# Order of the first chunk: tile 3's scores behind tile 1's product with v, a lower pace of the channel mix, and tile 1's v ahead of the fourth block of w_k

## The chip, the cores and the metric

The kernel runs on one core of a Trainium2 chip. The metric is the device time of one execution in microseconds (us). The kernel before was timed in three runs; one further execution was recorded by the hardware profiler.

## What is computed

Four batches of eight heads, 768 positions, head width 64; a biased local attention, and on its output a gated channel mix over the 512 joined features. Inputs are float32 (the weights are given as 64-bit words that the kernel turns into float32 itself).

```python
scores = q @ k.T / 8 + bias        # bias: -slope[h] * distance
scores = where(keep, scores, -1e9) # keep: first 8 keys, or 0 <= i - j < 96
a = exp(scores - max); a = a / (sum(a) + 1e-9)
x = a @ v                          # joined over heads: (4, 768, 512)
x_prev = x shifted by one position
xk = mu_k * x + (1 - mu_k) * x_prev
xr = mu_r * x + (1 - mu_r) * x_prev
k = maximum(xk @ w_k, 0)           # w_k 512 x 1024
out = sigmoid(xr @ w_r) * ((k * k) @ w_v)   # w_r 512 x 512, w_v 1024 x 512
```

## The kernel before

The work is cut into 24 tiles of 128 positions (6 to a batch). A step of the main loop (L658 and after) handles one tile in four quarters, `hp` 0 to 3. For a tile the scores are computed on TensorE (`scores`), the softmax on three engines (`softmax`: VectorE adds the bias and takes the maximum at L375, ScalarE takes the exponential at L376, VectorE the sum plus 1e-9 and its reciprocal at L389 and L390, GpSimd scales at L393), then the result is transposed and multiplied by v. The product with v of a tile is issued two steps after its scores (`weighted`, L473 and L487); its copy into `x` is at L496. Tiles 0 to 3 (`HEAD` is 4) use plain 128-key blocks, are transposed on TensorE (L453) and take their data from tiles loaded at the start; later tiles use a window of 168 keys, are transposed on VectorE (L410, L411) and go through a small DRAM buffer.

Two tiles make a chunk of 256 positions for the channel mix, 12 chunks in all (0 to 11). `ffn(c)` mixes x with its shifted copy (xk and xr; for chunk 0 in `plain_mix`, ScalarE at L521 and VectorE at L522) and returns a generator, `channel_mix`, whose parts are issued turn by turn: kp (x by w_k, L564), z (x by w_r, L542), vps (the squares by w_v, L597). Chunk 0 multiplies whole float32 words; the later chunks split each number into a high and a low part and use three products (L533 to L535). A budget counts the turns that the main loop grants: `run_ffn(2.5)` twice in each quarter, and -17.5 at the start of chunk 0, which is queued in step 3 (`LAG`).

The weights are 20 blocks of 128 x 512: 8 of w_k, 4 of w_r, 8 of w_v. `weight_load` issues the DMA of a block (L163, 0.5 MB) into a place named by `w_homes`, which must be free of its earlier use. `weight_begin` makes a float32 word of it: one step on ScalarE (even blocks, L178) or GpSimd (odd ones, L176) and three on VectorE (L179 to L181). `weight_split` makes the high part (ScalarE at L188, or GpSimd) and the low part (VectorE, L190 or L197) for the chunks after the first. `w_due` says how many blocks are loaded and begun by each quarter.

The order of instructions on each engine comes from a planner that takes the program's order as priority and its own estimate of times; `tc.issue_after(ins)` holds every instruction of a block that is on the engine of `ins` behind `ins`. Every engine works through its instructions in order. SyncE (SP) issues the DMAs in its own order.

Of the kernel before, what the change touches and what calls it, by code (L numbers as in the profile page):

```python
# [35 lines left out]
def tile_biased_attention_channel_mix(ctx: ExitStack, tc: tile.TileContext, qT, kT, v, n_sizes, mu_kr, w_k, w_v, w_r, q_rows, k_rows, v_rows, slopes, out):  # L36
# [108 lines left out]
    w_steps = [(name, src, k, c) for name, src, kts, n in (("k", w_k, 4, DF), ("r", w_r, 4, DM), ("v", w_v, 8, DM)) for c in range(0, n, 512) for k in range(kts)]  # L145

    w_raw = {}
    w_due = ((2, 3, 4, 5, 6, 6, 7, 7, 8, 8, 9, 9, 10, 11, 12, 13, 14, 16, 18, 20, 20, 20, 20, 20), (0, 1, 2, 3, 4, 4, 5, 5, 6, 6, 7, 7, 8, 8, 9, 10, 11, 12, 14, 16, 18, 20, 20, 20))

    def weight_load(i):  # L150
        name, src, k, c = w_steps[i]
# [12 lines left out]
        w_raw[i] = raw  # L164

    w_both = {}
    w_homes = ["xk_hi", "xr_hi", "xk_lo", "xr_lo", "kk_hi", "kk_hi", "kk_lo", "kk_lo"] + 2 * ["t4k", "t4k", "t4k", "xk_lo", "xr_lo"] + ["kk_lo", "kk_lo"]

    def weight_begin(i):
        name, src, k, c = w_steps[i]  # L170
# [12 lines left out]
    def weight_split(i):  # L183

        name, src, k, c = w_steps[i]
        word, hi = w_word.pop((name, k, c)), w_hi[name][:, k, c : c + 512]
        lo = w_low[name, k, c] = w_pool.tile([128, 512], F32R, tag="wl", name=f"w{name}_lo_{i}")
        (act.copy if i % 4 < 2 else pool_copy)(hi, word)  # L188
        if not gates:
            vec.tensor_sub(lo, word, hi)  # L190
        else:
            with ExitStack() as behind:
                if i == 8:
                    hold.extend(gates[-1:] + freed[-2:])
                for ins in hold or gates[-1:]:
                    behind.enter_context(tc.issue_after(ins))
                vec.tensor_sub(lo, word, hi)  # L197

    w_count = [0, 0, 0]
    marks = {}  # L200

    def weights_load(n):
        while w_count[2] < min(n, len(w_steps)):
# [2 lines left out]

    def weights_go(begun):
        weights_load(begun)
        with ExitStack() as behind:
            for ins in marks.values():  # L210
                behind.enter_context(tc.issue_after(ins))
            while w_count[0] < min(begun, len(w_steps)):
                weight_begin(w_count[0])
                w_count[0] += 1

    def splits_go(n):
        while w_count[1] < n:
# [5 lines left out]


    state = {}
    seen = {}
    room = r_pool.tile([128, 12, 512], F32, name="room")
    turned = room[:, 4:7].rearrange("p b x -> p (b x)").rearrange("p (l x) -> p l x", l=6)
    landed = room[:, 0:4].rearrange("p a (k x) -> p a k x", k=2)
# [73 lines left out]
    def window_tables():  # L303
        misc = q_pool.tile([128, 1024], F32, name="misc", tag="qh")
        table = q_pool.tile([128, H, WIN], BF16, name="patw", tag="qh")
        pool.memset(misc[0:32, 0:512], 0.0)
        pool_copy(table[:, :, 0:GMAX], pat[:, :, 0:GMAX])
        pool_copy(table[0:64, :, GMAX:WIN], pat[0:64, :, 32:192])
        pool_copy(table[64:128, :, GMAX:WIN], pat[64:128, :, 96:256])
        return misc[0:32, 0:512], misc[:, 512 : 512 + HH * GMAX].rearrange("p (h k) -> p h k", h=HH), table  # L310

    def scores(n, hp):
# [49 lines left out]
    def softmax(n, hp, j, units, w, p):  # L362
        s = state[n]
        for i, ps in units:
            for u in range(2):
                h = 2 * i + u
                o = ps[:, u * 256 : u * 256 + w]
                if n >= HEAD:
                    slot = 8 + 2 * j + i // 2
                elif n < HEAD - 3:  # L370
                    slot = 5 + (4 * (n - HEAD + 4) + 3 + i) % 7
                else:
                    slot = i + (4 if (HEAD - n) % 2 else 8)
                e = room[:, slot, 256 * u : 256 * u + 256]
                seen_max = vec.tensor_tensor_reduce(out=e[:, :w], in0=o, in1=p[:, h, :], op0=ALU.add, op1=ALU.min, scale=-0.125, scalar=3.0e38, accum_out=s["nmax"][:, h : h + 1])  # L375
                act.activation(e[:, :w], e[:, :w], AF.Exp, bias=s["nmax"][:, h : h + 1], scale=-1.0, accum_out=s["sum"][:, h : h + 1])  # L376
                s["e"][h] = e
        if n >= HEAD and j:
            freed.append(seen_max.ins)
        if j is None and hp % 2 == 0:  # L380
            return
        r = s_pool.tile([128, 4], F32, name=f"r_{n}_{hp}_{j}", tag="r", bufs=8)
        if j is not None:
            heads = (2 * j, 2 * j + 1, 2 * j + 4, 2 * j + 5)
            total = s["sum"].rearrange("p (a j u) -> p j a u", a=2, j=2)[:, j]
        else:
            heads = range(2 * hp - 2, 2 * hp + 2)
            total = s["sum"][:, 2 * hp - 2 : 2 * hp + 2].rearrange("p (a u) -> p a u", a=2)
        vec.tensor_scalar(r.rearrange("p (a u) -> p a u", a=2), total, 1.0e-9, None, op0=ALU.add)  # L389
        vec.reciprocal(r, r)  # L390
        for i, h in enumerate(heads):
            e = s["e"][h]
            pool.tensor_scalar(e[:, :w], e[:, :w], r[:, i : i + 1], 1.0, op0=ALU.mult, op1=ALU.mult)  # L393

    def turn(n, j):
        if n < HEAD:
# [60 lines left out]
    def weighted(n, hp):  # L457
# [6 lines left out]
        if n < HEAD:  # L464
            blocks = [state[n - 1]["va"], s["va"]] if t else [s["va"]]
            nb = len(blocks)
            et = s.pop(("et", hp))
            for u in range(2):
                h = 2 * hp + u
                o = s["av"][64 * u : 64 * u + 64, hp * 128 : (hp + 1) * 128]  # L470
                for k, vt in enumerate(blocks):
                    c = (u * nb + k) * 128
                    pe.matmul(o, vt[:, h * 64 : (h + 1) * 64], et[:, c : c + 128], start=k == 0, stop=k == nb - 1)  # L473
        else:
            lo, hi = slice(0, 64), slice(64, 128)
            every, own, back = slice(0, 4), 1, 0
            first, second = [("va", own, every), ("vb", back, slice(0, 2))], [("vb", back, every), ("va", own, slice(2, 4))]
            if not t:
                first = second = [("va", own, every)]
            for k in range(len(first)):  # L480
                for u in range(2):
                    h = 2 * hp + u
                    c = 32 * (HH * (hp % 2) + 2 * (hp // 2) + u)
                    for rows, bank, parts in ((lo, "av", first), (hi, "av2", second)):
                        vt, kind, a = parts[k]
                        o = s[bank][64 * u : 64 * u + 64, hp * 128 + 32 * a.start : hp * 128 + 32 * a.stop]
                        pe.matmul(o, s[vt][rows, h * 64 : h * 64 + 64], landed[rows, a, kind, c : c + 32], start=k == 0, stop=k == len(first) - 1)  # L487
# [28 lines left out]
    def plain_mix(xc, xp, tag):  # L516

        m, m1 = mu[tag]
        x = f_pool.tile([128, 4, 256], F32, name=f"x{tag}_0", tag=f"x{tag}_hi")
        for j in range(4):  # L520
            act.activation(x[:, j, :], xp[:, j, :], AF.Copy, scale=m1[:, j : j + 1])  # L521
            vec.scalar_tensor_tensor(x[:, j, :], xc[:, j, :], m[:, j : j + 1], x[:, j, :], op0=ALU.mult, op1=ALU.add)  # L522
        return x

    def channel_mix(xk, xr, out_rows, f_pool, f2_pool, ps_f, first=False, last=False):
# [11 lines left out]
        def z_of(i):  # L537
            z = ps_f.tile([128, 512], F32, name="z", tag="f")
            c = slice(i * 128, (i + 1) * 128)
            for k in range(4):  # L540
                if first:
                    pe.matmul(z, xr[:, k, c], w_word["r", k, 0], start=k == 0, stop=k == 3)  # L542
                else:
                    three(z, xr[0][:, k, c], xr[1][:, k, c], w_hi["r"][:, k, :], w_low["r", k, 0], k == 0, k == 3)
                    splits_ok[0] = len(w_steps)
# [5 lines left out]
        for fp in range(4):  # L551
# [17 lines left out]
                        yield  # L569
            kk = f2_pool.tile([128, 2, 256], F32, name="kk", tag="f2")  # L570
            pv = ps.rearrange("p (a q) -> p a q", a=2)
            act.activation(kk, pv, AF.Relu)  # L572
            if first:
                vec.tensor_mul(kk_all[:, 2 * fp : 2 * fp + 2, :], pv, kk)
            else:
# [33 lines left out]

    splits_ok = [0]  # L610
    gates = []
    freed = []
    hold = []
    waiting = []

    def ffn(c):
# [4 lines left out]
        elif c:  # L621
            xk, xr = (mix(xt[:, :, 1:257], xt[:, :, 0:256], tag, p4k, f_pool) for tag in "kr")
        else:
            xk, xr = (plain_mix(xt[:, :, 1:257], xt[:, :, 0:256], tag) for tag in "kr")
        return channel_mix(xk, xr, lambda i: out[(2 * c + i) * 128 : (2 * c + i + 1) * 128, :], f_pool, f2_pool, ps_f, c == 0, c == NCHUNK - 1)


    LAG = 3
    queue = []
    budget = [0.0]  # L630

# [15 lines left out]
    for step in range(NTILES + 1):  # L647
        if step + 2 < HEAD:
            load_tile(step + 2)
        if step < NTILES:  # L650
            load_v(step)
        if step == HEAD - 1:
            vg, kg, patw = window_tables()
        for hp in range(4):
            if hp == 0 and step > 1:
                for i in range(4):
# [4 lines left out]
                    receive(step - 1)  # L661
                transposes(step - 1, hp)
            if step < NTILES:
                if step < HEAD or hp == 0:
                    scores(step, hp)
                if hp > 1:
                    turn(step, hp - 2)
                if hp == 3:
                    send(step)
            if hp == 0:  # L670
                if step >= LAG and (step - LAG) % 2 == 0:
                    queue.append(ffn((step - LAG) // 2))
                    if len(queue) == 1 and step == LAG:
                        budget[0] = -17.5
            run_ffn(2.5)
            run_ffn(2.5)
            if hp == 1 and HEAD <= step + 1 < NTILES:
                load_tile(step + 1)
            if hp == 1 and step + 1 < NTILES:
                start_tile(step + 1)  # L680
            slot = 4 * step + hp
            weights_load(w_due[0][min(slot, 23)])
            weights_go(w_due[1][min(slot, 23)])
            marks.update(seen)
    for i in range(4):
        weighted(NTILES - 1, i)
    for c in range((NTILES - LAG) // 2 + 1, NCHUNK):
# [170 lines left out]
```

## Time and profile before

| what | us |
|---|---|
| median of 3 runs | 455.19 |
| lowest and highest of them | 454.78, 455.25 |
| the profiled execution | 456.54 |
| its span in the profile | 454.80 |
| TensorE busy in it | 440.2 (97%) |
| VectorE, ScalarE, GpSimd busy | 315.7, 264.5, 182.4 |

The span goes from the first to the last instruction; the profiled execution's own time is 1.74 us longer. The ends of matmuls are modelled, so a busy TensorE is not one at its peak. Times within the profile count from the start of the span.

### The profile page before, as it was taken

What the parts mean: (1) busy time and instruction counts of PE and PEld (TensorE: products, weight loads), DVE (VectorE), ACT (ScalarE), POOL (GpSimd) and SP (SyncE); (2) the same over time, 40 slices, a digit from 0 to 9 for tenths busy, and PEclk for the clock granted to TensorE, in tenths of its full rate; (3) what the DMA queues carried; (4) which work ended last, traced back from release to release, by engine and by line L of the source; (5) the groups of instructions that cost most, each with busy time, mean ns of one, the idle gap of its engine ahead of it and who ended that gap; (6) DMA issues with size and microseconds to landing.
All of it is one profiled execution on the core that took longest, in us unless ns stands there. A gap on an engine that the chain in (4) does not pass through costs nothing.

```text
span 454.8 us, 11244 instructions
## 1 busy us (share of the span) xinstructions
PE 440.2 (97%) x4066; PEld 374.2 (82%) x4066; DVE 315.7 (69%) x918; ACT 264.5 (58%) x638; POOL 182.4 (40%) x357
## 2 busy tenths in 40 slices
PE   7897999999999999999999999999999999999995
PEld 6775864687798898898898898898898898988985
DVE  6889999899786686666676676766766666637311
ACT  5978565546667466377468366466569359242220
POOL 8987655632524324424325224424425225204000
PEclk9988999999999999999999999999999999999999
DMA  5999968387478885787587785679487563520001
GB/s 168 273 320 257 257 198 224 83 220 208 75 210 209 199 239 155 161 223 195 107 221 204 172 242 149 143 212 228 111 230 211 138 187 94 126 85 25 23 2 51
DMA packets 72141, 77.75 MB, mean 171 GB/s; under 512 B 9296, under 2 KB 57680, under 8 KB 72080
## 3 DMA queue, kind: packets, MB, share of 16 engines
q1 hardware_dynamic: 71936, 76.97, 63.6%
q8 instruction: 34, 0.56, 0.5%
q14 instruction: 27, 0.22, 0.2%
q10 hardware_dynamic: 144, 0.00, 0.0%
HBM read 54.60 MB, written 21.23 MB: 167 GB/s over the span
## 4 chain that ended last, share of the span: by engine, by line
PE 75%; DVE 11%; DMA 6%; ACT 3%; issue 2%; POOL 2%; SPq 1%; DVEq 0%; POOLq 0%; ACTq 0%
PE kp L533 9%; PE kp L534 9%; PE kp L535 9%; PE vps L534 8%; PE vps L533 8%; PE vps L535 8%; PE av L487 6%; PE z L533 4%; PE z L534 4%; PE s L333 4%; PE z L535 4%; DMA qz<-in_qT_dram 3%; DMA w<-in_w_v_dram 2%; DVE word L180 2%; ACT room L376 1%
## 5 line engine op out<-in xcount | busy, mean ns | idle before, releaser
L393 POOL TENSOR_SCALAR room<-room,r 128x168 f32<-128x168 f32 (+1 forms) x160 | 76.0, 495 | 76.0 <-DVE r L390 41.4
L533 PE MATMUL kp<-xk_hi,wk_hi 128*128 128x256 f32 x352 | 99.5, 283 | 0.6 <-DVE x L498 0.6
L534 PE MATMUL kp<-xk_lo,wk_hi 128*128 128x256 f32 x352 | 98.3, 279 | 0.9 <-DVE xk_lo L511 0.7
L535 PE MATMUL kp<-xk_hi,wk_lo 128*128 128x256 f32 x352 | 98.6, 280 | 0.0
L376 ACT ACTIVATE room<-room,nmax 128x168 f32<-128x168 f32 (+2 forms) x192 | 82.0, 429 | 16.6 <-DVE nmax L375 16.4
L507 POOL TENSOR_SCALAR mix_k<-x,mus 128x256 f32<-128x256 f32 x44 | 24.8, 582 | 118.9 <-DVE x L498 114.9
L534 PE MATMUL vps<-wv_lo,kk_hi 128*128 128x512 f32 (+1 forms) x184 | 71.3, 387 | 0.0
L533 PE MATMUL vps<-wv_hi,kk_hi 128*128 128x512 f32 (+1 forms) x184 | 71.1, 387 | 0.0
L535 PE MATMUL vps<-wv_hi,kk_lo 128*128 128x512 f32 (+1 forms) x184 | 70.5, 383 | 0.0
L533 PEld LDWEIGHTS kp<-xk_hi,wk_hi 128*128 128x128 f32 x352 | 67.0, 190 | 4.0 <-issue 1.4
L534 PEld LDWEIGHTS kp<-xk_lo,wk_hi 128*128 128x128 f32 x352 | 65.9, 187 | 1.8 <-DVE xk_lo L511 1.0
L535 PEld LDWEIGHTS kp<-xk_hi,wk_lo 128*128 128x128 f32 x352 | 65.9, 187 | 0.0
L496 ACT COPY x<-av 128x512 f32<-128x512 f32 x24 | 14.1, 585 | 56.8 <-PE av L487 56.3
L577 ACT CAST kk_hi<-kk 128x512 fp32r<-128x512 f32 x44 | 27.1, 621 | 32.3 <-DVE kk L576 32.3
L498 DVE TENSOR_TENSOR x<-av,x 128x512 f32<-128x512 f32 x20 | 13.8, 690 | 44.6 <-ACT x L496 44.6
L533 PEld LDWEIGHTS vps<-wv_hi,kk_hi 128*128 128x128 f32 x184 | 34.6, 188 | 8.0
L535 PEld LDWEIGHTS vps<-wv_hi,kk_lo 128*128 128x128 f32 x184 | 34.5, 188 | 7.8
L534 PEld LDWEIGHTS vps<-wv_lo,kk_hi 128*128 128x128 f32 x184 | 34.5, 188 | 7.3
L572 ACT ACTIVATE kk<-kp 128x512 f32<-128x512 f32 x48 | 27.9, 591 | 19.9 <-PE kp L535 18.7
L578 DVE TENSOR_TENSOR kk_lo<-kk,kk_hi 128x512 fp32r<-128x512 f32 x44 | 29.4, 682 | 14.2 <-ACT kk_hi L577 13.7
L576 DVE TENSOR_TENSOR kk<-kp,kk 128x512 f32<-128x512 f32 x44 | 29.3, 678 | 10.5 <-ACT kk L572 9.9
L375 DVE CUSTOM_DVE_ANT_0 room<-s,patw 128x168 f32<-128x168 f32 x136 | 36.4, 324 | 0.0
(121 smaller groups left out, 941.9 us busy)
## 6 DMA issues: line engine op xcount, KB each, us to landing
moved<-room SPq DMA_DIRECT2D x68, 192.0 KB, 3.8
k<-in_k_rows_dram SPq DMA_DIRECT2D x68, 160.0 KB, 4.3
out_dram<-sig SPq DMA_DIRECT2D x23, 256.0 KB, 2.7
va<-in_v_dram SPq DMA_DIRECT2D x21, 256.0 KB, 4.3
q<-in_qT_dram SPq DMA_DIRECT2D x40, 128.0 KB, 4.5
room<-moved SPq DMA_DIRECT2D x34, 128.0 KB, 3.1
room<-moved SPq DMA_DIRECT2D x17, 256.0 KB, 3.6
w<-in_w_k_dram SPq DMA_DIRECT2D x8, 512.0 KB, 9.2
```

The costliest lines, as they stand in the source:

```text
L375: seen_max = vec.tensor_tensor_reduce(out=e[:, :w], in0=o, in1=p[:, h, :], op0=ALU.add, op1=ALU.min, scale=-0.125, scalar=3.0e38, accum_ou ...
L376: act.activation(e[:, :w], e[:, :w], AF.Exp, bias=s["nmax"][:, h : h + 1], scale=-1.0, accum_out=s["sum"][:, h : h + 1])
L393: pool.tensor_scalar(e[:, :w], e[:, :w], r[:, i : i + 1], 1.0, op0=ALU.mult, op1=ALU.mult)
L487: pe.matmul(o, s[vt][rows, h * 64 : h * 64 + 64], landed[rows, a, kind, c : c + 32], start=k == 0, stop=k == len(first) - 1)
L507: pool.tensor_scalar(tmp[:, j, :], xp[:, j, :], m1[:, j : j + 1], 1.0, op0=ALU.mult, op1=ALU.mult)
L533: pe.matmul(o, sh, mh, start=first, stop=False)
L534: pe.matmul(o, sh, ml, start=False, stop=False)
L535: pe.matmul(o, sl, mh, start=False, stop=last)
L572: act.activation(kk, pv, AF.Relu)
L576: vec.tensor_mul(kk, pv, kk)
L577: act.copy(kkh[:, 2 * fp : 2 * fp + 2, :], kk)
L578: vec.tensor_sub(kkl[:, 2 * fp : 2 * fp + 2, :], kk, kkh[:, 2 * fp : 2 * fp + 2, :])
```

## The change

Seven things change, all in the first steps.

- Tile 1's v is loaded in the third quarter of step 0, after three blocks of w_k instead of after five and tile 3's data. Blocks 3 to 5 are loaded one quarter later each. Blocks 4 and 5 and those from 8 on get other homes.
- The words of blocks 0 to 3 are begun in the last quarter of step 1, and `w_pins` puts the steps of blocks 0 to 5 behind named instructions of tiles 1 and 2.
- The splits' high parts come behind chunk 0's third relu (ScalarE) or tile 3's last scaling (GpSimd).
- Two copies of the bias table for windows go from GpSimd to the DMA queue; the rest of the tables comes behind tile 2's last scaling on GpSimd.
- Chunk 0 is queued before tile 3's scores instead of after them. Tile 3's scores are held behind tile 1's last product with v on TensorE, and its maxima behind the last xk mix on VectorE.
- The budget of chunk 0 starts at -6 instead of -17.5, and steps 3 and 4 grant 1.78 instead of 2.5.
- xr of chunk 0 is mixed at the end of step 3, behind tile 3's last exponential on ScalarE.

```diff
-    w_due = ((2, 3, 4, 5, 6, 6, 7, 7, 8, 8, 9, 9, 10, ...), (0, 1, 2, 3, 4, 4, 5, 5, 6, 6, 7, 7, 8, 8, 9, 10, ...))
+    w_due = ((2, 3, 3, 4, 5, 6, 7, 7, 8, 8, 9, 9, 10, ...), (0, 0, 0, 0, 0, 0, 0, 4, 4, 5, 6, 6, 7, 8, 9, 10, ...))
-    w_homes = ["xk_hi", "xr_hi", "xk_lo", "xr_lo", "kk_hi", "kk_hi", "kk_lo", "kk_lo"] + 2 * ["t4k", "t4k", "t4k", "xk_lo", "xr_lo"] + ["kk_lo", "kk_lo"]
+    w_homes = ["xk_hi", "xr_hi", "xk_lo", "xr_lo", "t4k", "t4k", "kk_lo", "kk_lo"] + ["t4k", "xk_lo", "xr_lo", "t4k", "t4k", "t4k", "xk_lo", "xr_lo", "kk_lo", "kk_lo", "t4k", "t4k"]
...
-        (act.copy if i % 4 < 2 else pool_copy)(hi, word)
+        with tc.issue_after(relus[2] if i % 4 < 2 else state[HEAD - 1]["scaled"]):
+            (act.copy if i % 4 < 2 else pool_copy)(hi, word)
...
+    w_pins = {
+        0: ((1, ("max", 3)), (1, ("exp", 3))),
+        1: ((1, ("rec", 3)), (1, ("scaled", 1))),
+        2: ((1, ("rec", 3)), (1, ("exp", 3))),
+        3: ((1, ("rec", 3)), (1, ("scaled", 3))),
+        4: ((2, ("max", 1)), (2, ("exp", 0))),
+        5: ((2, ("max", 1)), (2, ("scaled", 1))),
+    }
...
+        while w_count[0] < min(begun, len(w_steps)):
+            with ExitStack() as behind:
+                for n, what in w_pins.get(w_count[0], ()):
+                    behind.enter_context(tc.issue_after(state[n][what].ins))
                 weight_begin(w_count[0])
...
-        pool_copy(table[0:64, :, GMAX:WIN], pat[0:64, :, 32:192])
-        pool_copy(table[64:128, :, GMAX:WIN], pat[64:128, :, 96:256])
+        nc.sync.dma_start(table[0:64, :, GMAX:WIN], pat[0:64, :, 32:192])
+        nc.sync.dma_start(table[64:128, :, GMAX:WIN], pat[64:128, :, 96:256])
...
-            xk, xr = (plain_mix(xt[:, :, 1:257], xt[:, :, 0:256], tag) for tag in "kr")
+            xk, xr = plain_mix(xt[:, :, 1:257], xt[:, :, 0:256], "k"), late_r
...
-        if step < NTILES:
+        if step < NTILES and step != 1:
             load_v(step)
         if step == HEAD - 1:
-            vg, kg, patw = window_tables()
+            with tc.issue_after(state[HEAD - 2]["scaled"]):
+                vg, kg, patw = window_tables()
...
-                if step < HEAD or hp == 0:
+                if hp == 0 and step == LAG:
+                    queue.append(ffn(0))
+                    first_mixed = mixed[-1]
+                    budget[0] = -6.0
+                if step == LAG:
+                    with tc.issue_after(state[1]["done"].ins), tc.issue_after(first_mixed.ins):
+                        scores(step, hp)
+                elif step < HEAD or hp == 0:
                     scores(step, hp)
...
-                if step >= LAG and (step - LAG) % 2 == 0:
+                if step > LAG and (step - LAG) % 2 == 0:
                     queue.append(ffn((step - LAG) // 2))
-                    if len(queue) == 1 and step == LAG:
-                        budget[0] = -17.5
-            run_ffn(2.5)
-            run_ffn(2.5)
+            pace = 2.5 if step > LAG + 1 else 1.78
+            run_ffn(pace)
+            run_ffn(pace)
+            if hp == 3 and step == LAG:
+                with tc.issue_after(state[step]["exp", 3].ins):
+                    late_r.append(plain_mix(xt[:, :, 1:257], xt[:, :, 0:256], "r"))
...
+            if slot == 2:
+                load_v(1)
             weights_load(w_due[0][min(slot, 23)])
```

The remaining lines of the diff only record instructions under names (`s["max", hp]`, `s["exp", hp]`, `s["rec", hp]`, `s["scaled", hp]`, `s["done"]`, `mixed`, `relus`) or drop names that were unused.

## Rows read from the trace of the kernel before

**Rows 1.** The profile's page: the span in 40 slices, engines and DMA.

```profile
DVE  6889999899786686666676676766766666637311
...
DMA  5999968387478885787587785679487563520001
```

**Rows 2.** Windows: busy us of each engine, TensorE clock, DMA share, GB/s.

```profile
10.00:37.60 27.60, 22.37 (x181) 18.67 (x179) 24.18 (x85) 23.87 (x76) 22.56 (x34) 0.94 1.02 288
37.60:84.20 46.60, 46.45 (x256) 30.30 (x256) 42.26 (x108) 29.79 (x71) 30.84 (x47) 0.96 0.82 222
84.20:94.40 10.20, 9.33 (x130) 8.48 (x129) 10.13 (x18) 1.54 (x3) 2.88 (x5) 1.00 0.42 106
```

**Rows 3.** Waits of PE, 37 us to the end: waiter, releaser, total us, times, longest.

```profile
PE kp L564 <- DVE xk L522: 1.8, 1, 1.8
...
PE s L333 <- DVE kk L576: 0.2, 1, 0.2
```

**Rows 4.** Timeline of PE: start us, us, instruction, count, idle before it.

```profile
22.14 0.44 PE L453 MATMUL t<-ident,room 128*128 128x128 f32 x2 [1.40 <-POOL room L393]
...
24.11 0.62 PE L341 MATMUL s<-ring,qz 128*128 128x128 f32 x2 [0.81 <-DMA qz<-in_qT_dram]
...
28.32 1.53 PE L473 MATMUL av<-room,early 128*64 128x128 f32 x22
...
37.69 5.41 PE L564 MATMUL kp<-xk,word 128*128 128x256 f32 x16 [1.77 <-DVE xk L522]
```

**Rows 5.** Timeline of POOL, the first two tiles' scaling.

```profile
13.90 2.88 POOL L222 TENSOR_SCALAR patw<-pat 128x64 bf16<-128x64 bf16 x3 [0.26 <-POOL room L393]
16.88 2.32 POOL L393 TENSOR_SCALAR room<-room,r_None 128x256 f32<-128x256 f32 x4
19.17 1.16 POOL L176 TENSOR_SCALAR word<-w 128x512 f32<-128x512 f32 x1
...
21.38 3.25 POOL L393 TENSOR_SCALAR room<-room,r_None 128x256 f32<-128x256 f32 x4
```

**Rows 6.** Timeline of DVE, where it waits and three steps of the path.

```profile
15.85 1.21 DVE L179 TENSOR_SCALAR word<-word 128x512 int32<-128x512 int32 x1 [1.04 <-ACT word L178]
...
20.41 0.17 DVE L390 RECIPROCAL r_None<-r_None 128x4 f32<-128x4 f32 x1
...
27.67 0.42 DVE L375 CUSTOM_DVE_ANT_0 room<-s,pat 128x256 f32<-128x256 f32 x1 [1.23 <-PE s L342]
...
45.58 1.58 DVE L179 TENSOR_SCALAR word<-word 128x512 int32<-128x512 int32 x2 [0.55 <-POOL word L176]
...
77.80 0.68 DVE L181 SCALAR_TENSOR_TENSOR word<-w,word 128x512 int32<-128x512 int32 x1
...
83.31 0.22 DVE L389 TENSOR_SCALAR r<-sum 128x4 f32<-128x4 f32 x1 [2.05 <-ACT room L376]
```

**Rows 7.** Groups of DVE by line and form, 10 to 94.4 us.

```profile
L181 DVE SCALAR_TENSOR_TENSOR word<-w,word 128x512 int32<-128x512 int32 x20 | 14.3, 720 | 0.0
L180 DVE SCALAR_TENSOR_TENSOR word<-w,word 128x512 int32<-128x512 int32 x20 | 14.0, 712 | 0.0
L179 DVE TENSOR_SCALAR word<-word 128x512 int32<-128x512 int32 x20 | 12.3, 626 | 3.3 <-ACT word L178 2.1 <-POOL word L176 1.1
```

**Rows 8.** Timeline of ACT: tile 1's last exp, chunk 0's mix, a late weight.

```profile
16.88 0.19 ACT L376 ACTIVATION_READ_ACCUMULATOR room<-room,nmax 128x1 f32 x1
...
33.52 1.71 ACT L521 ACTIVATE xk<-x,mus 128x256 f32<-128x256 f32 x4
...
63.47 1.26 ACT L178 ACTIVATE word<-w 128x512 f32<-128x512 f32 x2 [1.73 <-DMA w<-in_w_v_dram]
```

**Rows 9.** Timeline of SP: DMA issues.

```profile
9.46 3.05 SPq L163 DMA_DIRECT2D w<-in_w_k_dram  x5
12.55 0.86 SPq L251 DMA_DIRECT2D qz<-in_qT_dram  x1
...
16.37 0.33 SPq L276 DMA_DIRECT2D early<-in_v_dram  x1
```

More of the change, by code (lines that the diff above doesn't have):

```diff
@@ L147, in tile_biased_attention_channel_mix @@
     w_raw = {}
-    w_due = ((2, 3, 4, 5, 6, 6, 7, 7, 8, 8, 9, 9, 10, 11, 12, 13, 14, 16, 18, 20, 20, 20, 20, 20), (0, 1, 2, 3, 4, 4, 5, 5, 6, 6, 7, 7, 8, 8, 9, 10, 11, 12, 14, 16, 18, 20, 20, 20))
+    w_due = ((2, 3, 3, 4, 5, 6, 7, 7, 8, 8, 9, 9, 10, 11, 12, 13, 14, 16, 18, 20, 20, 20, 20, 20), (0, 0, 0, 0, 0, 0, 0, 4, 4, 5, 6, 6, 7, 8, 9, 10, 11, 12, 14, 16, 18, 20, 20, 20))
     def weight_load(i):
@@ L199, in tile_biased_attention_channel_mix @@
     w_count = [0, 0, 0]
-    marks = {}
+    w_pins = {
[6 more added lines that the diff above has]
+    }
     def weights_load(n):
@@ L208, in weights_go @@
         weights_load(begun)
[L209 to L212, printed above, removed]
+        while w_count[0] < min(begun, len(w_steps)):
+            with ExitStack() as behind:
+                for n, what in w_pins.get(w_count[0], ()):
+                    behind.enter_context(tc.issue_after(state[n][what].ins))
                 weight_begin(w_count[0])
-                w_count[0] += 1
+            w_count[0] += 1
     def splits_go(n):
@@ L225, in tile_biased_attention_channel_mix @@
     state = {}
-    seen = {}
+    mixed = []
     room = r_pool.tile([128, 12, 512], F32, name="room")
@@ L374, in softmax @@
                 e = room[:, slot, 256 * u : 256 * u + 256]
-                seen_max = vec.tensor_tensor_reduce(out=e[:, :w], in0=o, in1=p[:, h, :], op0=ALU.add, op1=ALU.min, scale=-0.125, scalar=3.0e38, accum_out=s["nmax"][:, h : h + 1])
-                act.activation(e[:, :w], e[:, :w], AF.Exp, bias=s["nmax"][:, h : h + 1], scale=-1.0, accum_out=s["sum"][:, h : h + 1])
+                seen_max = s["max", hp] = vec.tensor_tensor_reduce(out=e[:, :w], in0=o, in1=p[:, h, :], op0=ALU.add, op1=ALU.min, scale=-0.125, scalar=3.0e38, accum_out=s["nmax"][:, h : h + 1])
+                s["exp", hp] = act.activation(e[:, :w], e[:, :w], AF.Exp, bias=s["nmax"][:, h : h + 1], scale=-1.0, accum_out=s["sum"][:, h : h + 1])
                 s["e"][h] = e
@@ L389, in softmax @@
         vec.tensor_scalar(r.rearrange("p (a u) -> p a u", a=2), total, 1.0e-9, None, op0=ALU.add)
-        vec.reciprocal(r, r)
+        s["rec", hp] = vec.reciprocal(r, r)
         for i, h in enumerate(heads):
             e = s["e"][h]
-            pool.tensor_scalar(e[:, :w], e[:, :w], r[:, i : i + 1], 1.0, op0=ALU.mult, op1=ALU.mult)
+            s["scaled", hp] = pool.tensor_scalar(e[:, :w], e[:, :w], r[:, i : i + 1], 1.0, op0=ALU.mult, op1=ALU.mult)
+        s["scaled"] = s["scaled", hp].ins
     def turn(n, j):
@@ L472, in weighted @@
                     c = (u * nb + k) * 128
-                    pe.matmul(o, vt[:, h * 64 : (h + 1) * 64], et[:, c : c + 128], start=k == 0, stop=k == nb - 1)
+                    s["done"] = pe.matmul(o, vt[:, h * 64 : (h + 1) * 64], et[:, c : c + 128], start=k == 0, stop=k == nb - 1)
         else:
@@ L521, in plain_mix @@
             act.activation(x[:, j, :], xp[:, j, :], AF.Copy, scale=m1[:, j : j + 1])
-            vec.scalar_tensor_tensor(x[:, j, :], xc[:, j, :], m[:, j : j + 1], x[:, j, :], op0=ALU.mult, op1=ALU.add)
+            mixed.append(vec.scalar_tensor_tensor(x[:, j, :], xc[:, j, :], m[:, j : j + 1], x[:, j, :], op0=ALU.mult, op1=ALU.add))
         return x
@@ L541, in z_of @@
                 if first:
-                    pe.matmul(z, xr[:, k, c], w_word["r", k, 0], start=k == 0, stop=k == 3)
+                    pe.matmul(z, xr[0][:, k, c], w_word["r", k, 0], start=k == 0, stop=k == 3)
                 else:
@@ L571, in channel_mix @@
             pv = ps.rearrange("p (a q) -> p a q", a=2)
-            act.activation(kk, pv, AF.Relu)
+            relus.append(act.activation(kk, pv, AF.Relu).ins)
             if first:
@@ L611, in tile_biased_attention_channel_mix @@
     gates = []
+    relus = []
     freed = []
@@ L623, in ffn @@
         else:
-            xk, xr = (plain_mix(xt[:, :, 1:257], xt[:, :, 0:256], tag) for tag in "kr")
+            xk, xr = plain_mix(xt[:, :, 1:257], xt[:, :, 0:256], "k"), late_r
         return channel_mix(xk, xr, lambda i: out[(2 * c + i) * 128 : (2 * c + i + 1) * 128, :], f_pool, f2_pool, ps_f, c == 0, c == NCHUNK - 1)
     LAG = 3
+    late_r = []
     queue = []
@@ L681, in tile_biased_attention_channel_mix @@
             slot = 4 * step + hp
+            if slot == 2:
+                load_v(1)
             weights_load(w_due[0][min(slot, 23)])
             weights_go(w_due[1][min(slot, 23)])
-            marks.update(seen)
     for i in range(4):
```

## Prediction

> **What bounds the kernel now.** I read the page's slices first [rows 1]. VectorE's digits are mostly 8 and 9 up to the tenth slice and 6 or 7 afterwards; the DMA engines are at 9 from the second to the fifth slice. So the first 100 us are another stage than the rest. From there on TensorE simply works through its queue. The waits of TensorE say the same: after 37 us five of them are named, from 1.8 down to 0.2 us, 3.6 us together [rows 3]. Whatever the change gains must therefore come from starting chunk 0's channel mix earlier than 37.69 us, and it is kept only if VectorE and the DMA queue feed the earlier start.
>
> The windows give both margins [rows 2]. Before 37.6 us TensorE is busy for 22.37 of 27.60 us at a granted clock of 0.94 (1.00 being 2.4 GHz): 5.2 us idle, and 0.06 x 27.6 = 1.7 us lost to the clock. With the 3.6 us of later waits this is at most 10.5 us that TensorE could give. VectorE is idle for 3.4 us there, for 4.3 us up to 84.2 us and for 0.1 us up to 94.4 us: 7.8 us in all, and this is the smaller margin. The DMA share is 1.02 at 288 GB/s before 37.6 us.
>
> Then the start of chunk 0, back from its first matmul at 37.69 us, which waits 1.77 us for VectorE's mix [rows 4]. The mix waits for ScalarE at 33.52 [rows 8], this for tile 1's product with v, most of which runs at 28.32, behind tile 3's scores, which wait for their q until 24.11 [rows 4]. That q is queued behind five blocks of w_k, and tile 1's v comes after it, at 16.37 [rows 9]. Tile 1's second half is scaled on GpSimd only at 21.38, because the table copies hold that engine from 13.90 for 2.88 us and weight words stand between [rows 5]; its reciprocal comes at 20.41 [rows 6], though its last exp has ended at 17.07 [rows 8].
>
> **The change, part by part.** *The start of chunk 0.* With the table copies on the DMA queue and the words pinned behind, tile 1's last exp ends at about 16.4 (17.07 less one word step on ScalarE, estimated at 1.26 / 2 = 0.63 from [rows 8]); a reciprocal of 0.17 [rows 6] and its sum before it give 16.9; scaling at the 2.32 us of the first half [rows 5] gives 19.2; transposes of 0.44 [rows 4] and a copy bring tile 1 to about 20. Its v now goes out after three blocks. A block is 0.5 MB, 1.8 us at 288 GB/s; word 0 became usable at 15.15 (its VectorE step at 15.85 less 0.7 on ScalarE), so blocks 1 and 2 and v arrive at about 17.0, 18.8 and 19.7. The product with v (1.53 us for most of it [rows 4]) is over at about 21.5, x and ScalarE's 1.71 us [rows 8] at about 24. But the first matmuls also want words 0 to 3: 0.626 + 0.712 + 0.720 = 2.06 us each on VectorE [rows 7], 8.2 us from 17, with tile 2's eight maxima (0.42 us each [rows 6], 3.4 us) in between. That is 25 to 29 us; I take 27.5, ten microseconds ahead of 37.69.
>
> *Ten at the start are not ten at the end.* Twenty words take 14.3 + 14.0 + 12.3 = 40.6 us of VectorE before 94.4 us [rows 7], and no edit takes one away. The last ends at 77.80 + 0.68 = 78.5 [rows 6], and the products with w_v need it. What VectorE saves is only its idle time, and I go through it [rows 6]. The 1.04 us at 15.85 (first word) can be filled with tile 2's maxima: gain 1.0. The 1.23 us at 27.67 is tile 3's scores, whose q was late; they now stand behind work that is ready: 1.2. The 0.55 us at 45.58 is a word on GpSimd queued behind scaling; its successor is pinned elsewhere: 0.5. The words at about 56, 60 and 64 us wait for w_v itself, as ScalarE does at 63.47 for 1.73 us [rows 8]; a faster VectorE would wait longer there, so nothing is gained. The 2.05 us at 83.31 wait for ScalarE's exps; no edit touches them directly, I take 0 (bounds: all of it gone, or as much again). The first word step shrinks from 1.21 to the mean 0.63 if it was slow because GpSimd copied tables beside it [rows 5 to 7]: 0.6, bounds 0 and 0.8.
>
> *The table copies* move 2 x 64 x 8 pieces of 320 bytes, 0.33 MB, on a full queue: 1.1 us at 288 GB/s [rows 2]. Hidden (0) if the queue has slack before w_v is wanted; 1.1 if it delays every block after it. I take 0.3, nearer to nothing, since DMA is at 0.82 after 37.6 us. The Trainium skill, "DMA: Bandwidth & Descriptors", Specifications, states that transfers want at least 512 bytes for line rate and that shorter ones cost a read-modify-write. If that doubled the time, it would be an estimated 2.3 us instead of 1.1; no row here has such a copy.
>
> *The rest costs nothing by itself.* The lower pace only spreads the same 40 turns of chunk 0: from -6, 16 turns of 1.78 in two steps leave 22.5, as -17.5 with 2.5 did. Splitting the weights behind the third relu and tile 3's scaling frees ScalarE and GpSimd early; its cover is that the lower halves are wanted only by chunk 1 at 84 us, and without that cover one costs about 0.7 us. Mixing xr behind tile 3's exps is covered by the sixteen kp groups ahead of z. The new homes of blocks 4 and 5 only move which block waits for which. Behind the fourth xk mix now wait tile 3's maxima, and behind these its exps, scaling and product with v.
>
> *Sum:* 1.0 + 1.2 + 0.5 + 0.6 - 0.3 = 3.0 us. The profiled execution took 456.54 us (span 454.80 and 1.74 around it), so 453.5; it is 1.35 us above the median of 455.19, so 452.2 on the median's scale.
>
> **The rivals.** *(a) More is gained.* If the 83.31 wait goes too, and VectorE has no idle time but the 0.8 us that precede the first word, 7 us go: 448.2. For it: TensorE's margin of 10.5 us allows it. Against: w_v's arrival does not move.
>
> *(b) The gain is hidden.* The channel mix starts early and then waits for w_v, whose blocks arrive when they did, less what 1.02 of share leaves, which is nothing. If the queue moves the small table pieces ahead of w_v at half of the 288 GB/s, 0.33 MB takes 2.3 us, and the 3.3 us of gains leave 1.0: 454.2; with the 1.2 us of tile 3's scores not gained either, 455.2, no change. (This is what the Trainium skill's rule above, on the same page and section, would make of the copies.) For it: ScalarE's 1.73 us wait at 63.47 [rows 8]. Against: between the last block's arrival and 78.5 VectorE had a backlog, so arrival did not set the end.
>
> *(c) Slower.* Tile 3's maxima are now behind the fourth mix of xk on an engine that works in order. If tile 1's x is late, VectorE runs out: the words 0 to 3 and tile 2's maxima last from 17 to 29, words 4 and 5 until 33. From a mix later than 33 on, it decides: at the 35.2 us at which ScalarE now ends the mix [rows 8], 2.2 us idle, and the 3.4 us of maxima come behind it, on the way to the words of w_v, so that instead of 3.0 gained 2 are lost: 457.2. For it: the chain through five engines moves only if each link does. Against: each link has a reason above.
>
> **How the numbers follow.** This kernel's three runs lie within 0.1% of their median, so 0.2% (0.9 us) is about what can be told from no change. The forecast (gain 1.5 to 5) has 0.50, (a) 0.18, (b) 0.16, half of it within 0.2%, (c) 0.16. Faster is 0.50 + 0.18 + 0.04 = 0.72, the same 0.10, slower 0.14 + 0.04 = 0.18. The likeliest is 452.2, its own range 450.2 to 453.7; the range for 8 in 10 goes from 447.7, just past (a), to 456.2, half of (c).
>
> **What would show it.** Right: kp's first matmul at 25 to 30 us; tile 1's second scaling before 18; VectorE's idle time before 94.4 us at about 5 us; the last word at about 75. Wrong: a first matmul after 33; a VectorE wait of 2 us or more on tile 3's scores; words of w_v that wait for DMA longer than before by as much as chunk 0 is earlier; new TensorE waits in the products with w_v.

## The result, and the profile after

| what | before | after |
|---|---|---|
| median of the timed runs, us | 455.19 (5 runs, 454.19 to 455.58) | 460.12 (5 runs, 458.18 to 460.77) |
| profiled execution, us | 456.54 | 460.38 |
| its span, us | 454.80 | 458.6 |

The change makes the kernel slower: the ratio is 1.0099, with a 95% interval of 1.0082 to 1.0116, which is 4.5 us; the medians differ by 4.9. 452.2 was forecast and the range ended at 456.2.

The page's slices of after stand beside [rows 1]: the clock has a digit of 7 in the fifth slice (46 to 57 us), and VectorE has a 6 there where it had a 9.

```profile
DVE  6899699599786775765676685766675666637311
...
PEclk9999799999999999999999999999999999999999
DMA  6999985476658885787577785678478773430001
```

The windows of after, cut where the trace changes, answer to [rows 2] (columns as there).

```profile
10.00:37.60 27.60, 25.11 (x199) 20.94 (x199) 25.08 (x83) 22.64 (x72) 18.80 (x31) 1.00 0.99 299
37.60:42.60 5.00, 4.99 (x53) 4.14 (x51) 5.00 (x16) 2.35 (x7) 3.99 (x6) 1.00 1.11 220
42.60:46.80 4.20, 0.04 (x1) 0.07 (x2) 3.65 (x10) 3.39 (x10) 1.33 (x2) 1.00 1.04 237
46.80:55.00 8.20, 8.20 (x34) 6.25 (x34) 5.04 (x17) 2.60 (x10) 3.33 (x5) 0.58 1.05 281
55.00:60.00 5.00, 5.00 (x32) 4.25 (x31) 4.09 (x13) 2.87 (x6) 5.00 (x8) 1.00 0.76 229
60.00:84.20 24.20, 24.20 (x118) 12.40 (x116) 21.18 (x55) 17.18 (x43) 18.12 (x27) 1.00 0.71 187
84.20:94.40 10.20, 10.20 (x113) 7.34 (x113) 7.31 (x13) 1.64 (x2) 3.42 (x10) 1.00 0.31 80
```

Up to 37.6 us TensorE does what was hoped for: idle 2.5 us instead of 5.2, and the clock 1.00 instead of 0.94, which together is 4.4 us gained. Then it stands still for 4.2 us and afterwards runs 8.2 us at 0.58, near the lower of its two levels (1.2 GHz would be 0.50): 8.2 x 0.42 = 3.4 us more. Before had 2.0 us of both from 37.6 to 84.2 [rows 2], so these two alone give back 5.6.

What it stands for is in the timeline of TensorE (columns as in [rows 4]).

```profile
29.02 1.03 PE L573 MATMUL kp<-xk,word 128*128 128x256 f32 x4
...
38.59 1.46 PE L573 MATMUL kp<-xk,word 128*128 128x256 f32 x6
...
46.76 3.30 PE L341 MATMUL s<-k,q 64*64 64x168 f32 x20 [4.17 <-DMA k<-in_k_rows_dram]
49.98 4.96 PE L573 MATMUL kp<-xk,word 128*128 128x256 f32 x12
```

Chunk 0 begins at 29.02 instead of 37.69 [rows 4], but half of its 64 kp matmuls stand behind the first 20 of tile 4's score matmuls, and these want tile 4's keys. (The expectations below count kp's matmuls in pairs, 32 in all.) The twelve kp matmuls behind them take 4.96 us; at full clock twelve took 2.86 in the kernel before, where tile 4's scores ran in one go and without a wait:

```profile
45.41 2.63 PE L333 MATMUL s<-k,q 64*64 64x168 f32 x32
47.97 2.86 PE L564 MATMUL kp<-xk,word 128*128 128x256 f32 x12
```

SyncE's timeline of after, and its waits from 30 to 62 us, say why the keys are late; the last fence is the same issue in the kernel before.

```profile
34.27 0.67 SPq L316 DMA_DIRECT2D patw<-pat  x1
34.99 0.63 SPq L317 DMA_DIRECT2D patw<-pat  x1
...
41.38 3.37 SPq L271 DMA_DIRECT2D k<-in_k_rows_dram  x4
```

```profile
SPq L271 <- DMA patw<-pat: 1.0, 2, 0.7
```

```profile
41.07 2.58 SPq L263 DMA_DIRECT2D k<-in_k_rows_dram  x4
```

The consumer moved forward, and the keys did not: they are issued at 41.38, as late as before. Two things hold them. Their home (`ring`) comes free with tile 3's scores, which the tie moved behind tile 1's product with v: the last of them runs at 38.37. And two of the key loads wait for the table copies, issued eight DMAs earlier: 7 us pass between the first copy's issue and the first key's. In this order of issues the copies are what ends the wait: the home had been free since 38.8, and SyncE still waited 0.7 us for the first copy just before 41.38. Without the copies the home decides (number 2). Seven us is not special to small pieces. Whole blocks of w_r, 512 KB each, took as long from issue to landing in these stretches (25 to 60 us), after and before:

```profile
w<-in_w_r_dram SPq DMA_DIRECT2D x3, 512.0 KB, 6.9
```

```profile
w<-in_w_r_dram SPq DMA_DIRECT2D x3, 512.0 KB, 7.8
```

VectorE's timeline shows the end of chunk 0, later than in [rows 6].

```profile
79.67 1.28 DVE L181 SCALAR_TENSOR_TENSOR word<-w,word 128x512 int32<-128x512 int32 x2
...
87.09 0.69 DVE L613 TENSOR_TENSOR sig<-vps,sig 128x512 f32<-128x512 f32 x1 [5.11 <-PE vps L606]
```

VectorE waits 5.11 us there for the last products with w_v. These stand in TensorE's timeline, of the kernel before and of after:

```profile
77.69 6.60 PE L597 MATMUL vps<-word,kk 128*128 128x512 f32 x15
```

```profile
85.07 3.70 PE L606 MATMUL vps<-word,kk 128*128 128x512 f32 x8
```

They end at 84.29 and at 88.77: chunk 0 is 4.5 us late, and the spans differ by 3.8. It is TensorE that is late. From 46.8 to 94.4 it has no idle time in the windows above, so VectorE's last word, at 80.95, did not hold it.

The new order costs TensorE once more. Before, tile 3's product with v and tile 5's scores stood one behind the other, 3.3 us together:

```profile
64.99 0.45 PE L473 MATMUL av<-room,early 128*64 128x128 f32 x4
...
66.94 1.37 PE L333 MATMUL s<-k,q 64*64 64x168 f32 x32
68.24 1.98 PE L542 MATMUL z<-word,xr 128*128 128x512 f32 x4
```

After, the same matmuls mix, and between 65.37 and 74.04 they take 4.9 us without the two groups of z among them, 1.7 us more:

```profile
65.37 0.43 PE L482 MATMUL av<-room,early 128*64 128x128 f32 x2
...
68.88 0.50 PE L341 MATMUL s<-k,q 64*64 64x168 f32 x2
69.31 0.45 PE L482 MATMUL av<-room,early 128*64 128x128 f32 x4
...
70.92 1.36 PE L341 MATMUL s<-k,q 64*64 64x168 f32 x28
72.22 1.98 PE L551 MATMUL z<-word,xr 128*128 128x512 f32 x4
74.04 10.46 PE L606 MATMUL vps<-word,kk 128*128 128x512 f32 x24
```

### The profile page after: what moved, and what is told of

Its sections match the earlier page's. It is cut to its first block, busy times and chain, and to the rows that moved or that the text cites. A ratio compares the mean times of both kernels' runs of the same rounds, so it can differ in the third digit from the quotient of the medians.

```text
span 458.6 us, 11233 instructions
## 1 busy us (share of the span) xinstructions
PE 444.3 (97%) x4066; PEld 375.5 (82%) x4066; DVE 312.9 (68%) x918; ACT 262.0 (57%) x636; POOL 179.1 (39%) x355
## 4 chain that ended last, share of the span: by engine, by line
PE 84%; DMA 5%; DVE 4%; SPq 2%; ACT 1%; POOL 1%; issue 1%; ACTq 0%; POOLq 0%
PE kp L542 9%; PE kp L543 9%; PE kp L544 8%; PE vps L543 8%; PE vps L542 8%; PE vps L544 8%; PE av L496 6%; PE s L341 6%; PE z L542 4%; PE z L543 4%; PE z L544 4%; PE kp L573 3%; PE vps L606 3%; DMA qz<-in_qT_dram 2%; PE z L551 2%; DMA w<-in_w_k_dram 2%
## 5 line engine op out<-in xcount | busy, mean ns | idle before, releaser
L401 POOL TENSOR_SCALAR room<-room,r 128x168 f32<-128x168 f32 (+1 forms) x160 | 77.2, 500 | 77.1 <-DVE r L398 49.6
L507 DVE TENSOR_TENSOR x<-av,x 128x512 f32<-128x512 f32 x20 | 13.8, 689 | 44.1 <-ACT x L505 44.1
L542 PEld LDWEIGHTS vps<-wv_hi,kk_hi 128*128 128x128 f32 x184 | 34.6, 188 | 8.0
```

Source lines behind the costliest of these rows:

```text
L401: s["scaled", hp] = pool.tensor_scalar(e[:, :w], e[:, :w], r[:, i : i + 1], 1.0, op0=ALU.mult, op1=ALU.mult)
L542: pe.matmul(o, sh, mh, start=first, stop=False)
```

## The experiments

Theory: TensorE works in order, meets tile 4's scores before their keys have landed, and pays twice, for the wait and for the clock after it. Rivals: VectorE's last words of w_v set the end of chunk 0; the copies cost DMA time as such; the tie, the early v or the splits' places cost by themselves. The planner writes every engine's order anew for each kernel, so an edit can also move instructions far from itself; where that mattered it is said. Ratios are to the kernel before, with 95% intervals. What an edit gives back is told as a difference of medians; by the ratios the change costs 4.5 us, and numbers 2 and 6 give back 2.8 and 2.9 of them.

**1. Pace 2.5 in all steps** (chunk 0's products ahead of tile 4's scores).

```diff
-            pace = 2.5 if step > LAG + 1 else 1.78
+            pace = 2.5
```

> The changed kernel with the pace of 2.5 in all steps instead of 1.78 in steps 3 and 4; the budget still starts at -6. All 32 kp products of chunk 0 then stand ahead of tile 4's scores in TensorE's order, instead of 16. Theory A (TensorE stands 4.2 us before tile 4's scores because their keys land at 46.6 us and nothing is queued ahead, then runs at half clock to 55 us): the wait falls under 1 us, the clock stays at 1.0 from 42 to 55 us, and the time falls by 5 to 8 us to 452 to 455. Rival B (the table copies on the DMA queue delay keys and weights): no more than 1 us off 460. Rival C (the tie makes tile 3's scores late, and with them the keys and the last blocks of w_v): chunk 0 still ends near 88 us and the time stays at 458 to 461.

498.53 us, 1.0912 (1.0834 to 1.0991). TensorE's longest waits, over the span:

```profile
PE av L496 <- ACT xk_hi L518: 5.0, 4, 1.5
PE kp L543 <- DVE xk_lo L520: 4.3, 3, 1.7
...
PE s L341 <- DMA k<-in_k_rows_dram: 0.5, 1, 0.5
```

The wait for the keys went, as the theory says, but the expectation missed by 44 us. The budget at the end of step 4 was 34 turns instead of 22.5, so each later chunk was issued 11.5 turns earlier against its tiles and, as the waits for `xk_hi` and `xk_lo` say, met its mix too early, chunk after chunk. The budget has to be kept when the pace is changed. Number 6 does that, with the same pace in step 3, and the 42 us are gone.

**2. The table copies back on GpSimd.**

```diff
-        nc.sync.dma_start(table[0:64, :, GMAX:WIN], pat[0:64, :, 32:192])
-        nc.sync.dma_start(table[64:128, :, GMAX:WIN], pat[64:128, :, 96:256])
+        pool_copy(table[0:64, :, GMAX:WIN], pat[0:64, :, 32:192])
+        pool_copy(table[64:128, :, GMAX:WIN], pat[64:128, :, 96:256])
```

> The changed kernel with the two table copies on GpSimd again. Theory A: tile 4's keys are issued about 1 us earlier, since their issue waited 1.0 us for the copies, and land at 45.5; the wait of TensorE is 3 us instead of 4.2; time 458 to 459.5. Rival B: keys and the last blocks of w_v land 2 us or more earlier and the time is back at 455 to 456.

456.63 us, 1.0038 (1.0016 to 1.0059): 3.5 us of the 4.9 come back, more than theory A had, which left 3 us of the wait. The keys are issued at 39.20, when tile 3's last scores have freed their home, tile 4's scores start at 43.67 without a wait, and the clock stays whole (timeline of SyncE, of TensorE, window):

```profile
39.20 3.02 SPq L271 DMA_DIRECT2D k<-in_k_rows_dram  x4
```

```profile
43.67 2.10 PE L341 MATMUL s<-k,q 64*64 64x168 f32 x20
45.70 2.86 PE L573 MATMUL kp<-xk,word 128*128 128x256 f32 x12
```

```profile
46.80:55.00 8.20, 8.20 (x50) 6.63 (x49) 8.20 (x32) 5.61 (x17) 3.58 (x7) 1.00 1.06 269
```

**3. Tile 3's scores untied**, that is, issued as before the change.

```diff
-                if step == LAG:
-                    with tc.issue_after(state[1]["done"].ins), tc.issue_after(first_mixed.ins):
-                        scores(step, hp)
-                elif step < HEAD or hp == 0:
+                if step < HEAD or hp == 0:
```

> The changed kernel without the tie: tile 3's scores are free to stand before tile 1's product with v and their maxima before the mix. Theory A: still 16 of 32 kp products stand ahead of tile 4's scores, so TensorE still waits there, by as much as the keys land after about 42 us: 457 to 460. Rival C: the home of the keys is free about 10 us earlier, the keys land before 42 us, no wait, 454 to 456.

461.06 us, 1.0118 (1.0081 to 1.0154), no better than the change. The wait for the keys shrank to 0.8 us (the first two are issued at 36.84), but VectorE's words came later: the last is begun at 83.63, and a wait of 3.0 us for them in the products with w_v. So the tie costs the keys their early home; that it also keeps words in front on VectorE, and that the one is worth about the other, is the likely reading and was not tested by itself.

**4. Tile 1's v and the blocks of w_k loaded in the order of before.**

```diff
-        if step < NTILES and step != 1:
+        if step < NTILES:
...
-            if slot == 2:
-                load_v(1)
```

> The changed kernel with tile 1's v and the blocks of w_k loaded at the places of before. Theory A: chunk 0 starts some 2 us later, at about 31 us, and this only shortens the wait for tile 4's keys; the time stays within 1 us of 460. If tile 1's early v were worth something by itself, the time would be 2 us or more above 460.

457.57 us, 1.0071 (1.0039 to 1.0104). kp starts at 31.85, tile 4's scores come due at 44.1 instead of 42.6, their keys (issued at 41.51) at 44.74, and the clock stays at 1.00 there. Earlier, at 22.5, TensorE stands 3.07 us for tile 1's v. The expectation (within 1 us of 460) was missed: by the medians the kernel is 2.5 us faster than the change although chunk 0 starts 2.8 us later. Its ten runs spread from 455.81 to 461.75, and the intervals of the two ratios overlap, so this gain is likely and not shown.

**5. The copies issued from ScalarE's queue** (`nc.scalar` for `nc.sync`); TensorE's order is that of the change, instruction by instruction.

> The changed kernel with the two table copies issued from ScalarE's DMA queue instead of SyncE's; TensorE's order is the same as in the changed kernel. If the copies cost by standing in SyncE's queue (tile 4's keys, eight issues behind the first copy, wait for it to land), the keys are issued at about 39 us instead of 41.4, TensorE no longer waits 4.2 us, and the time is near that with the copies on GpSimd: 456 to 457.5. If they cost by their bytes and small pieces, the keys land as late as before and the time stays at 459 to 460.5.

458.49 us, 1.0075 (1.0047 to 1.0104). The key loads are still held by the copies (4.0 us of SyncE's waits), the scores start at 46.27 after 2.15 us, and the clock in 46.8 to 55 is 0.68. Their place in SyncE's queue is therefore not the point: they land late wherever they are issued. With the same order on TensorE the stop is about half as long and the median lies 1.6 us lower, though the intervals overlap. The Trainium skill, "DMA: Bandwidth & Descriptors", Issuing engines are not separate DMA queues, states that transfers run on the same 16 DMA engines whichever engine starts them; this run agrees.

**6. Early pace with the budget kept** (2.5 in step 3, 1.06 in step 4; copies still on the DMA queue).

```diff
-            pace = 2.5 if step > LAG + 1 else 1.78
+            pace = 1.06 if step == LAG + 1 else 2.5
```

> The changed kernel with a pace of 2.5 in step 3 and 1.06 in step 4: the budget at the end of step 4 is the same 22.5, so the later chunks keep their phase, but all 32 kp products of chunk 0 stand ahead of tile 4's scores. Theory A (the wait at tile 4's scores and the half clock behind it): the wait falls under 1 us, the clock stays at 1.0 between 42 and 55 us, the time falls to 455.5 to 457.5 with the copies still on the DMA queue. If the end of chunk 0 is set by the last words of w_v whatever TensorE does before, it stays at 459 to 460.5. If the 38 us of the uniform pace of 2.5 come from something else than the phase of the later chunks, it is far above 465 again.

456.35 us, 1.0036 (1.0019 to 1.0054): 3.8 us come back with the copies left as they are. All 64 kp matmuls stand ahead of tile 4's scores, which wait 0.80 and 0.45 us, at a clock of 1.00 from 37.6 to 84.2. (The profiled execution took 460.35 us, 4 us above the median; it has a stop of another kind at 85 to 88 us, which number 9 shows.) Numbers 2 and 6 mend the same stop from its two ends, the keys and the order, and give the same.

**7. The kernel before with the copies on SyncE's queue alone.**

> The kernel before with the two table copies on SyncE's DMA queue and nothing else changed. If the copies delay tile 4's keys whatever stands around them: keys 2 us later than at 45.4, a wait of TensorE there, 457 to 458.5. If they cost only together with the tie of tile 3's scores: 454.5 to 456.

457.94 us, 1.0062 (1.0036 to 1.0087): this edit costs 2.8 us even where nothing else is changed. The time is as expected and the way is not. The keys are issued at 41.95 instead of 41.07, and TensorE names no wait for them at tile 4's scores. Its longest wait is another one, for GpSimd's scaling ahead of the transposes, here and in the kernel before:

```profile
PE t L453 <- POOL room L393: 6.9, 6, 2.3
```

```profile
PE t L453 <- POOL room L393: 2.5, 3, 1.4
```

The planner made another order of TensorE's and GpSimd's work here. How much of the 2.8 us is the copies' time on the DMA queue and how much this order is not shown.

**8. Number 2, and the splits' high parts free of their places** (the `issue_after` in `weight_split` removed).

> The changed kernel with the table copies on GpSimd and the splits' high parts free to come early again. If holding them behind the third relu and tile 3's scaling costs the remaining 1.3 us (low parts of w_k fall among the last words of w_v on VectorE at 58 to 68 us), the last word comes earlier than 80 us and the time is at 454 to 455.5. If not, 456.5 to 458.

463.49 us, 1.0189 (1.0160 to 1.0217). Free splits come in front: the xk mix is late by 3.4 us at kp, the keys are issued at 45.48 instead of 39.20, and the scores wait 6.3 us. Holding them back is worth 7 us here, and the expected gain was wrong.

**9 to 11. Combinations**: number 2 with 6 (9), 2 with 4 (10), and all three (11).

> The changed kernel with both suspected losses taken out: the two table copies are GpSimd's again, and the pace of the first chunk is 2.5 in step 3 and 1.06 in step 4 (the same 22.5 turns by the end of step 4), so that 28 of chunk 0's 32 products with w_k stand ahead of tile 4's scores. Theory (keys of tile 4 awaited by a TensorE that works in order, then half clock): both edits mend the same loss, so they do not add; no wait over 1 us at tile 4's scores, granted clock 1.00 from 40 to 60 us, and the time is that of the copies on GpSimd alone, 456.6 +- 0.8. Rival (two separate losses, DMA and order, each worth some 3 us): they add, chunk 0's products with w_v end by 82 us and the time is 453 to 454. Rival two (VectorE's words are the bound once the stop is gone): last words of w_v still end at 80 to 82 us, 455.5 to 457.

> The changed kernel with the copies on GpSimd and tile 1's v and the blocks of w_k loaded in the order of before; what is left of the change is the tie of tile 3's scores, the pins of the words, the splits' places, the late mix of xr, the homes and the pace. With tile 1's v late the first products with w_k start at about 31 to 32 us, as in the run with v late alone. Theory: the two edits both shorten the wait for tile 4's keys, which is already under 1 us after either, so together they give no more than the better: 456 to 457. Rival (the early v costs by itself, about 1.3 us, by holding back words of w_k or w_v): 454.5 to 455.5, level with the kernel before.

> All three together: copies on GpSimd, pace 2.5 in step 3 and 1.06 in step 4, tile 1's v and the blocks of w_k in the order of before. If the end of chunk 0 is set by VectorE's last words of w_v (80 to 82 us in each of the runs that took one part away), this too stays at 455.5 to 457. If each part has a loss of its own, the sum is some 452 to 453.5 and this beats both kernels.

460.06 us, 1.0108 (1.0079 to 1.0137); 458.30, 1.0072 (1.0046 to 1.0097); 459.02, 1.0078 (1.0049 to 1.0107). No expectation had this: each is slower than its better half. The combination 9 shows how. Its tile 4 scores never wait for keys, VectorE's last word ends at 76.35, and chunk 0's products end at 83.45; TensorE then comes to the product with v of tile 4, the first whose softmax weights make their way through two DMAs, `moved` and back (timelines of SyncE and TensorE, window). (The expectation of number 12 calls these tile 5's; tile 5's go out only at 88.62.)

```profile
79.74 2.37 SPq L430 DMA_DIRECT2D moved<-room  x4
83.31 3.02 SPq L439 DMA_DIRECT2D room<-moved  x5
```

```profile
88.10 0.69 PE L496 MATMUL av<-room 64*64 64x128 f32 x4 [3.28 <-DMA room<-moved]
```

```profile
85.00:95.00 10.00, 6.90 (x73) 6.03 (x77) 7.85 (x24) 1.93 (x5) 1.45 (x3) 0.66 0.73 197
```

The same stop and the same clock as at 42.6, 45 us later, for the next input that is not ready. In 10 it is tile 1's v (4.8 us, and the keys again with 2.7), in 11 tile 1's v too (4.4 us). The rival that VectorE's words close chunk 0 falls with 9 as well: they ended seven us before chunk 0's products did, and the time was no better.

**12. Number 2, tile 5's scores behind tile 3's product with v.**

```diff
+                elif step == 5 and hp == 0:
+                    with tc.issue_after(state[3]["done"].ins):
+                        scores(step, hp)
```

> The changed kernel with the table copies on GpSimd and, besides, tile 5's scores held behind tile 3's product with v, so that both stand whole in TensorE's order (the change let the two mix, which cost 1.7 us at 65 to 72 us). Theory (TensorE's order decides, and VectorE's last words of w_v close chunk 0): the mixing is mended, but the words of w_v still end at 80 to 82 us, so the time stays within 0.8 us of the copies on GpSimd alone, 455.8 to 457.4. Rival (TensorE's time in the products of chunk 0 is the bound): the 1.7 us come back and the time is 454.5 to 455.2. Third (whatever is put behind moves the next late input forward, here tile 5's turned weights at 85 to 89 us): a new wait of 2 to 4 us there with half clock after, 458 to 460, as in the run with copies on GpSimd and the early pace.

460.60 us, 1.0122 (1.0098 to 1.0145): the third case in kind, with a shorter wait than its 2 to 4 us. Both stand whole, and the first 24 of chunk 0's products with w_v run early; then TensorE waits 0.91 and 0.33 us for words and 1.29 us for tile 4's weights, and the last eight run at a reduced clock (5.15 us instead of 3.70):

```profile
82.05 0.60 PE L496 MATMUL av<-room 64*64 64x128 f32 x2 [1.29 <-DMA room<-moved]
82.58 5.15 PE L606 MATMUL vps<-word,kk 128*128 128x512 f32 x8
```

No version beat the kernel before.

## Why the prediction was wrong

**The early start was right.** kp's first matmul was forecast at 27.5 (25 to 29) and came at 29.02. Its first links held: tile 1's last exp ended at 16.28 (forecast 16.4), and its second scaling began at 17.57 (before 18). ScalarE's mix ended at 28.3 (forecast 24), which is why the start lies at the upper bound.

**VectorE's waits were half right.** The 1.23 us at 27.67 went. The 1.04 us at 15.85 went too, but 1.50 us for tile 2's scores stand at 16.33, and the 0.55 us at 45.58 is still there, at 44.52. The first word step did shrink, from 1.21 to 0.40 us. VectorE was busy for 25.08 us up to 37.6 instead of 24.18: 0.9 us more, of the 2.8 that these and the first word had been given.

**The step that failed is the bound.** "From there on TensorE simply works through its queue", and "this is the smaller margin" of VectorE's 7.8 us. The sum counted what chunk 0's own inputs (words, x, w_v) would allow and took TensorE's later waits as they were, 3.6 us, at most to be gained. But these waits were short because their inputs had been given time: with chunk 0 8.7 us earlier, the next thing in TensorE's order, tile 4's scores, comes due at 42.6 instead of 45.41, while the change moves its keys, if at all, to later. Numbers 2 and 6 show it: keys earlier, or scores later in the order, and 3.5 to 3.8 us of the 4.9 come back. VectorE's margin, from which the 3.3 us of gains were taken, did not bind: by the windows of after VectorE was idle for 13.05 us up to 94.4, where about 5 were forecast, and its last word ended at 80.95 instead of about 75, while TensorE worked without a pause from 46.8 on. The list of what would prove the forecast wrong looked for new waits in the products with w_v and not here.

**The table copies were mis-sized**: 0.3 us, with an upper bound of 1.1 by bytes over rate. Taking them off the DMA queue gave 3.5 us back (number 2); put there alone they went with a loss of 2.8 us, whose way is not shown (number 7). Bytes over rate is not what a DMA costs whose landing others wait for: it took some 7 us on a full queue, and the key loads stood behind it. Nor is it their time on the DMA engines: in the trace's records of single packets the 1024 pieces take 36 ns each, 2.3 us of all 16 engines. That is the price that rival (b) used.

**The clock was left out of the forecast.** The 0.94 before 37.6 was counted as something to gain, but that a new stop brings a half clock after it was in no rival. The Trainium skill, "TensorE: Matmul & The Clock Gate", What's actually happening, states that the engine falls to 1.2 GHz when it has been idle; the trace agrees, with 0.58 for 8.2 us after 4.2 us of standing. Not every stop here was followed by it (last section).

**Sums.** The margin of 10.5 us left out the clock of 0.96 from 37.6 to 84.2 [rows 2], 1.9 us. In rival (b), 3.3 less 2.3 and 1.2 is a loss of 0.2, so 455.4 and not 455.2; in (c), 3.0 less 2.2 and 3.4 is a loss of 2.6, so 457.8 and not 457.2. None of them changes the account.

**The rivals.** (c) had the sign and not the mechanism: the mix was on VectorE from 27.66 on, well before the 33 that was to decide. (b), a gain that is hidden, is nearest to what is left in numbers 2 and 6: the start is some 8 and 7 us earlier (29.39 and 30.87) and the time still 0.4% longer than before. Why these two stop there, and do not reach the kernel before, stays open; the profiles can hardly tell, since number 2's profiled execution has the same span as that of the kernel before, 454.8 us. Each single mend left a next input late (words at 80 to 82 us in 2, tile 4's weights in the profiled execution of 6), but mending two at once did not add up, and in 9, 11 and 12 the planner's order differs in many places at once. Of the 4.5 us by which chunk 0 ends later, the windows account for 5.6 - 4.4 = 1.2. The mixing of tile 3's product with tile 5's scores accounts for 1.7, and six scores of tile 6 that now stand ahead of the last eight products with w_v (84.43 to 85.07) for 0.6. The last 1.0 lies in stretches in which TensorE counts as busy and was not followed further.

## What to carry to other kernels

When work is moved forward on an engine that works in order, look at what stands behind it in that order, and when each of those inputs is issued and from which buffer: what was in time for the old order is late for the new one. A DMA is costed by when it lands and by who is queued behind its landing, not by its bytes alone. A pace that is tuned as a budget over steps must keep its sum, or every later stage shifts.

## What the runs showed of the hardware

One stop of TensorE can cost nearly double: 4.17 us of waiting were followed by 8.2 us at a granted clock of 0.58, in which 3.4 us of work were lost; in combination 9, 3.28 us of waiting lie in ten microseconds at 0.66. In the kernel before, the 1.77 us of [rows 4] are followed by 0.67 from 37.7 to 42.9. But the length of a stop alone does not decide. Waits of 0.80 and 0.45 us (number 6) and of 0.6 us (number 4) left the clock at 1.00, and so did 3.02 us in number 3 (timeline of TensorE, window) and 2.29 us at 34.6 in number 7; 1.29 us in number 12 were followed by the reduced clock. What else decides is not shown here.

```profile
75.59 1.98 PE L606 MATMUL vps<-word,kk 128*128 128x512 f32 x4 [3.02 <-DVE word L181]
```

```profile
70.00:88.00 18.00, 14.98 (x49) 6.11 (x48) 15.11 (x42) 7.07 (x21) 13.30 (x18) 1.00 0.54 134
```

And 0.33 MB of small copies between on-chip tables, 1.1 us by bytes over rate and 2.3 us of the DMA engines' time, kept other loads waiting for 7 us and more from their issue, from SyncE's queue and from ScalarE's alike; whole blocks of 512 KB took 6.9 and 7.8 us on the same queue.
